# A gated linear-attention kernel with a low-rank expert layer: all queues ordered anew, four more decayed k on GpSimd, and the first r and k requested on ScalarE's queue

## The chip, the core and the metric

The program runs on one core of a Trainium2 chip. A core has five engines that run their own instruction queues in order: TensorE (PE, matrix products into PSUM; its weight loads are listed as PEld), VectorE (DVE), ScalarE (ACT), GpSimd (POOL) and SyncE (SP, which in this kernel only requests transfers). Sixteen DMA engines move data between memory and SBUF. The engines meet through semaphores. The metric is device time in microseconds, one launch, median of the runs.

## The reference

Inputs are r, k, v, w of shape (4 batches, 8 heads, 768 steps, 48), u of shape (8, 48), and the expert layer's w_gate (384 x 8), A (8 x 384 x 16) and B (8 x 16 x 384). For each batch and head a 48 x 48 state is carried over the steps:

```
for t in range(768):
    cur   = outer(u * k[t], v[t])
    y[t]  = r[t] @ (state + cur)
    state = w[t][:, None] * state + outer(k[t], v[t])
```

The y of the 8 heads are laid side by side: x has 3072 tokens of 384 numbers. Each token picks its two experts with the largest x @ w_gate, softmaxes these two logits, and the output is x + sum over the two of weight * (x @ A[e]) @ B[e].

## The kernel before

The 768 steps of a batch are cut into six tiles of 128 steps, so there are 24 tiles, numbered 0 to 23; all 8 heads of a tile are treated together, as four pairs. The recurrence becomes matrix work within a tile and a state that is passed from tile to tile. A tile t goes through these stages (the names are functions inside `tile_kernel`, and a name with a number, such as kmul.5, is that stage for that tile):

- loads: `load_rk` (r and k, 514 KB, one of a ring of 12 buffers), `load_w` (two tiles at a time, except that tiles 0 and 1 come singly), `load_v` (the first three tiles by SP in float32, then cast by `castv`; the later ones by GpSimd's own queue, several tiles at a time), `consts` (0: u, 1: aw, the gate and A side by side, 2: B), which `castc` turns to bf16
- decay: `ln` (ACT, logarithm of w), `cs` (PE, cumulative sums into the one PSUM buffer x_ps), `expp` and `expm` (ACT, exponentials of the sums and of their negatives; `expm` overwrites x_ps, or writes an SBUF tile em where the product after it is GpSimd's)
- products: `rmul` (GpSimd, r times the decay, tile rd), `qmul` (GpSimd, r times k, tile q), `kmul` (k times the inverse decay, the "decayed k", on VectorE or, for the tiles in K_ON_POOL, on GpSimd)
- scores: `amm` (PE, into the one PSUM buffer a_ps), `aev` (VectorE, multiplies by the causal mask, the costliest stage there; tile 23 does it in two halves, `aev` and `aev2`), `dgmm` and `dv` (the diagonal term with u)
- state: `ktr`, `ktev` (decayed k transposed, and copied out), `kv` (PE, adds to the state s_ps), `resc` (VectorE, every second tile), `sev` (a copy of the state)
- output of the attention: `ymd`, `ymS`, `ymv` (PE), `yev` (copy to xT)
- expert layer: `zl` (PE, gate and A for three tiles together), `top`, `gexp`, `gsel`, `gmul`, `gnorm`, `gmul2`, `zw` (choice of the two experts), `zT`, `zTev`, then per tile `dmm` (PE), `oev` (copy to res) and `store` (SP)
- `warm.n`: n matmuls of zeros that fill PE's idle time

Which instruction follows which on every engine is written out by hand in the string ORDER (L53 to L99): the program is issued in this order, and an engine runs its own stages in the order in which they stand there. Constants above it (L41 to L50) tell which engine takes a stage that two could do: K_ON_POOL, KT_ON_DVE, S_ON_DVE, OUT_ON_DVE, ZT_ON_ACT, V_ON_ACT and so on; L166 to L176 are the copies. PE's, VectorE's, ACT's and GpSimd's queues and SP's requests are all set in this way. A request on SP also waits until the request eight places before it has landed.

Of the kernel before, what the change touches and what calls it, by code (L numbers as in the profile page):

```python
# [23 lines left out]
HD = H * D  # L24
# [3 lines left out]
WL = 2  # L28
# [15 lines left out]
V_ON_ACT = (0, 1)  # L44
K_ON_POOL = (8, 9, 14, 17, 21, 22, 23)
KT_ON_DVE = (0, 6, 13, 16, 20)
S_ON_DVE = (1, 8, 18, 21)
Y_ON_DVE = (20,)
OUT_ON_DVE = (2, 10, 23)
ZT_ON_ACT = (2, 14, 17, 20)  # L50
# [11 lines left out]
yev.3 kv.3 resc.3 sev.3 dgmm.4 dv.4 amm.4 aev.4 gmul2.2 zw.2 qmul.6 cs.6 expp.6 ktr.4 ktev.4 expm.6 kmul.6
rmul.6 ymd.4 ymS.4 kv.4 sev.4 ymv.4 yev.4 dgmm.5 dv.5 load_v.9 zT.2 zTev.2 amm.5 aev.5 cs.7 dgmm.6 dv.6
ymd.5 consts.2 castc.2 dmm.1 expp.7 expm.7 load_v.12 load_rk.7 qmul.7 rmul.7 kmul.7 load_w.8 load_rk.8 ln.8
qmul.8 load_rk.9 load_w.10 load_rk.10 load_rk.11 load_w.12 load_rk.12 ymS.5 ymv.5 yev.5 ktr.6 ktev.6 amm.6
aev.6 oev.1 store.1 cs.8 expp.8 expm.8 rmul.8 kmul.8 dmm.0 oev.0 store.0 load_rk.13 load_w.14 load_rk.14
load_rk.15 load_w.16 load_rk.16 load_rk.17 dgmm.7 dv.7 ymd.6 zl.5 ymv.6 yev.6 kv.6 sev.6 top.5 gexp.5 gsel.5
amm.7 aev.7 ktr.7 ktev.7 cs.9 expp.9 expm.9 dmm.2 oev.2 store.2 gmul.5 gnorm.5 qmul.9 ln.10 ymd.7 ymS.7
dgmm.8 dv.8 gmul2.5 zw.5 ymv.7 yev.7 kv.7 resc.7 sev.7 amm.8 aev.8 ktr.8 ktev.8 zT.5 zTev.5 kmul.9 ymd.8
cs.10 expp.10 expm.10 ymS.8 dgmm.9 dv.9 kv.8 sev.8 ymv.8 yev.8 kmul.10 rmul.9 amm.9 aev.9 qmul.10 qmul.11  # L70
ktr.9 ktev.9 dmm.4 oev.4 store.4 rmul.10 dmm.3 oev.3 store.3 cs.11 expp.11 expm.11 rmul.11 dgmm.10 dv.10
zl.8 top.8 gsel.8 kv.9 resc.9 kmul.11 ln.12 gexp.8 gmul.8 gnorm.8 gmul2.8 ymd.9 ktr.10 ktev.10 ymS.9 ymv.9
yev.9 amm.10 aev.10 sev.9 qmul.12 cs.12 expp.12 expm.12 rmul.12 qmul.13 dmm.5 oev.5 dgmm.11 dv.11 qmul.14
ymd.10 ymS.10 ymv.10 yev.10 kv.10 sev.10 kmul.12 amm.11 load_w.18 load_rk.18 load_rk.19 load_w.20 load_rk.20
dgmm.12 qmul.15 ln.14 cs.13 expp.13 expm.13 rmul.13 zw.8 zT.8 ymd.11 ymS.11 aev.11 ymv.11 amm.12 yev.11
store.5 dv.12 ktr.12 ktev.12 zTev.8 dmm.7 oev.7 dmm.6 oev.6 store.6 kmul.13 aev.12 dgmm.13 dv.13 cs.14
expp.14 expm.14 rmul.14 ln.16 zl.11 top.11 gexp.11 load_v.18 ymd.12 ktr.13 ktev.13 gsel.11 gmul.11 amm.13
aev.13 ymv.12 yev.12 kv.12 kmul.14 cs.15 gnorm.11 gmul2.11 dgmm.14 dv.14 qmul.17 ymd.13 sev.12 kv.13 ymS.13
resc.13 expp.15 expm.15 rmul.15 dmm.8 oev.8 store.8 kmul.15 zw.11 ymv.13 yev.13 qmul.16 ktr.14 ktev.14
amm.14 aev.14 cs.16 ymd.14 zT.11 zTev.11 dgmm.15 dv.15 qmul.18 sev.13 ymS.14 store.7 expp.16 expm.16 rmul.16  # L80
kmul.16 load_rk.21 load_w.22 kv.14 ymv.14 yev.14 amm.15 dmm.10 oev.10 store.10 ln.18 ktr.15 ktev.15 aev.15
ymd.15 sev.14 cs.17 expp.17 expm.17 kmul.17 zl.14 top.14 gexp.14 dgmm.16 dv.16 ymS.15 kv.15 resc.15 gsel.14
gmul.14 ymv.15 yev.15 amm.16 aev.16 rmul.17 sev.15 gnorm.14 gmul2.14 cs.18 expp.18 expm.18 rmul.18 ktr.16
ktev.16 qmul.19 dmm.9 oev.9 ymd.16 kmul.18 ln.20 zw.14 ymS.16 ymv.16 yev.16 dgmm.17 dv.17 qmul.20 dmm.11
oev.11 store.11 kv.16 sev.16 amm.17 aev.17 cs.19 expp.19 expm.19 rmul.19 dgmm.18 dv.18 qmul.21 ymd.17
kmul.19 zT.14 zTev.14 load_rk.22 load_rk.23 ymS.17 ymv.17 yev.17 amm.18 aev.18 ktr.18 ktev.18 dmm.12 cs.20
# [515 lines left out]
```

## Time and profile before

| what | value |
|---|---|
| time, median of 3 runs | 87.56 us (87.2 to 87.73) |
| the profiled execution | 87.54 us |
| its span in the profile | 85.7 us |
| PE busy | 77.1 us (90%) |
| VectorE busy | 73.1 us (85%) |
| ScalarE busy | 70.5 us (82%) |
| GpSimd busy | 61.9 us (72%) |
| moved by DMA | 25.43 MB, mean 297 GB/s |

The span runs from the first instruction to the last; the time has the launch around it. Busy time counts an engine's own instructions without requests of transfers, and the ends of PE's matmuls are modelled. The last loads are requested at 60.8 us, so that from about 64 us on only stores are left. A row of the timeline is: start in us, length in us, engine, line, operation, output <- input, shapes, count, and in square brackets the idle time of that engine just before and whom it waited for. Tile names in rows: lw is the logarithm, ep and x_ps the two exponentials, rd and q GpSimd's products, kd with a number a decayed k, at the masked scores, sb the copied state, idle_ps the output of a `warm` matmul.

### The profile page before, as it was taken

The numbers are of one execution on the slowest core, as the hardware profiler recorded it, in microseconds if no ns is written. First come the engines' busy times: TensorE is split into PE (matmuls) and PEld (weight loads), VectorE is DVE, ScalarE is ACT, GpSimd is POOL, SyncE is SP. The second block draws the span as 40 slices with busy tenths as digits, with TensorE's granted clock in tenths as the row PEclk, the third lists the DMA queues.
The fourth block names the chain that finished last, engine by engine and source line by source line (L and its number), as shares of the span: only waits on it lengthen the run. The fifth ranks groups of instructions, "written<-read, shape, count | busy, mean of one in ns | idle before, by whom it ended". The sixth has DMA issues, their size and how long they took to land.

```text
span 85.7 us, 3410 instructions
## 1 busy us (share of the span) xinstructions
PE 77.1 (90%) x1354; PEld 56.8 (66%) x1354; DVE 73.1 (85%) x176; ACT 70.5 (82%) x156; POOL 61.9 (72%) x88
## 2 busy tenths in 40 slices
PE   4899999979999999999989999999999999999810
PEld 1226557567676987787778877877787778675400
DVE  5946559969999999999999999999997999957830
ACT  5275887958999999999989989999999886976500
POOL 6054978698899798896987999499965897822000
PEclk9999999999999999999999999999999999999998
DMA  1999999999999999999999999999995504202461
GB/s 30 339 360 376 409 410 304 387 398 352 336 407 419 324 288 259 357 418 402 417 412 390 418 416 256 286 403 369 323 363 193 191 11 183 92 15 92 184 228 47
DMA packets 10384, 25.43 MB, mean 297 GB/s; under 512 B 1280, under 2 KB 4992, under 8 KB 10368
## 3 DMA queue, kind: packets, MB, share of 16 engines
q1 hardware_dynamic: 9648, 23.15, 70.7%
q0 software_dynamic: 720, 2.06, 12.1%
q8 instruction: 10, 0.16, 0.8%
q14 instruction: 6, 0.05, 0.2%
HBM read 22.56 MB, written 4.72 MB: 318 GB/s over the span
## 4 chain that ended last, share of the span: by engine, by line
DVE 34%; PE 24%; DMA 11%; ACT 8%; issue 8%; SPq 6%; POOL 4%; DVEq 0%; POOLq 0%; ACTq 0%
DMA aw_f<-in_aw_dram 11%; DVE at L314 10%; DVE dv L299 5%; PE a_ps L307 4%; DVE zw L474 3%; PE y_ps L371 3%; PE kd L281 3%; PE z_ps L412 3%; SPq L193 3%; DVE s_ps L339 2%; POOL rd L263 2%; SPq L187 2%; PE x_ps L240 2%; PE d_ps L512 2%; PE d_ps L496 2%
## 5 line engine op out<-in xcount | busy, mean ns | idle before, releaser
L263 POOL TENSOR_TENSOR rd<-rk,ep 128x512 bf16<-128x512 f32 x24 | 26.2, 1092 | 5.1 <-ACT ep L248 4.9
L314 DVE TENSOR_TENSOR at<-a_ps,mask 128x1024 bf16<-128x1024 f32 x23 | 28.0, 1218 | 1.7 <-PE a_ps L307 1.5
L258 POOL TENSOR_TENSOR q<-rk 128x384 bf16<-128x384 f32 x24 | 20.7, 866 | 2.8 <-DMA rk<-in_rk_dram 2.1
L248 ACT ACTIVATE ep<-x_ps 128x512 f32<-128x512 f32 x24 | 14.7, 614 | 2.5 <-PE x_ps L242 1.3
L170 ACT CAST xT<-y_ps 128x512 bf16<-128x512 f32 x22 | 13.1, 595 | 0.5 <-PE y_ps L371 0.2
L240 PE MATMUL x_ps<-tri,lw 128*128 128x128 f16 x96 | 12.0, 227 | 0.4 <-ACT lw L230 0.4
L230 ACT ACTIVATE lw<-w_in 128x768 f16<-128x768 f32 (+1 forms) x13 | 10.5, 806 | 1.4 <-DMA w_in<-in_w_dram 1.3
L299 DVE TENSOR_TENSOR dv<-v_bf,kd 128x384 bf16<-128x384 bf16 x21 | 11.4, 542 | 0.1
L170 ACT COPY res<-d_ps 128x384 f32<-128x384 f32 x21 | 9.9, 493 | 0.8 <-PE d_ps L512 0.7
L254 ACT ACTIVATE x_ps<-x_ps 128x512 f32<-128x512 f32 x17 | 10.4, 614 | 0.0
L240 PEld LDWEIGHTS <-lw 128*128 128x128 f16 x96 | 7.8, 100 | 3.0 <-ACT lw L230 1.7
L355 PE MATMUL y_ps<-ident,dv 128*128 128x128 bf16 x94 | 9.2, 219 | 0.1
L164 PE MATMUL idle_ps<-zero 128*128 128x512 bf16 x18 | 7.9, 560 | 1.2 <-DVE zero L111 1.2
L371 PE MATMUL y_ps<-at,v_bf 128*48 128x128 bf16 x160 | 8.1, 221 | 0.5 <-DVE at L314 0.4
L512 PE MATMUL d_ps<-b_b,zT 128*128 128x384 bf16 x24 | 7.8, 327 | 0.4 <-DVE zT L168 0.3
L364 PE MATMUL y_ps<-rd,sb 48*48 48x128 bf16 x156 | 8.0, 220 | 0.1
L496 PE MATMUL d_ps<-ident,xT 128*128 128x96 bf16 x92 | 7.7, 206 | 0.0
L170 ACT COPY ks<-kd 128x384 bf16<-128x384 bf16 x15 | 7.3, 488 | 0.3
L371 PEld LDWEIGHTS <-v_bf 128*48 128x48 bf16 x168 | 5.7, 101 | 2.2 <-issue 0.6
L242 PE MATMUL x_ps<-ones,lw 128*128 128x128 f16 x48 | 7.0, 227 | 0.0
L412 PE MATMUL z_ps<-aw_b,xT 128*128 128x136 bf16 x92 | 6.7, 222 | 0.0
L355 PEld LDWEIGHTS <-dv 128*128 128x128 bf16 x96 | 6.2, 97 | 0.6 <-DVE dv L299 0.3
(184 smaller groups left out, 158.9 us busy)
## 6 DMA issues: line engine op xcount, KB each, us to landing
rk<-in_rk_dram SPq DMA_DIRECT2D x24, 514.0 KB, 9.3
out_dram<-res SPq DMA_DIRECT2D x23, 192.0 KB, 4.2
w_in<-in_w_dram SPq DMA_DIRECT2D x11, 384.0 KB, 9.9
v_bf<-in_v_dram POOLq DMA_DIRECT2D x2, 576.0 KB, 10.1
v_bf<-in_v_dram POOLq DMA_DIRECT2D x3, 288.0 KB, 7.4
w_in<-in_w_dram SPq DMA_DIRECT2D x2, 192.0 KB, 3.2
v_f<-in_v_dram SPq DMA_DIRECT2D x1, 384.0 KB, 6.1
aw_f<-in_aw_dram SPq DMA_DIRECT2D x1, 272.0 KB, 9.3
```

Of the source, the lines that this page charges most:

```text
L170: nc.scalar.copy(out=o, in_=i)
L230: nc.scalar.activation(out=lw[:, o:o + n, :, 0:D].rearrange("p c h d -> p (c h) d"), in_=w_in[:, 0:n].rearrange("p c (h d) -> p (c h) d", ...
L240: nc.tensor.matmul(x_ps[:, p, :], lhsT=lwof(t, p), rhs=tri, start=True, stop=t % WL == 0)
L248: nc.scalar.activation(out=ep[:, :, o + 1:o + L + 1], in_=st[t]["x"], func=ACT.Exp)
L254: nc.scalar.activation(out=em, in_=st[t]["x"], func=ACT.Exp, scale=-1.0)
L258: (nc.vector if t in Q_ON_DVE else nc.gpsimd).tensor_mul(q, st[t]["r"][:, 0:PQ], st[t]["k"][:, 0:PQ])
L263: (nc.vector if t in R_ON_DVE else nc.gpsimd).tensor_mul(rd, st[t]["r"], st[t]["ep"][:, :, 0:L])
L299: nc.vector.tensor_mul(o[:, :, 0:D], vseq[t], dg.to_broadcast([128, H, D]))
L314: nc.vector.tensor_mul(at.rearrange("s g p f -> s (g p) f"), st[t]["a_ps"].rearrange("s g p f -> s (g p) f"), mask.to_broadcast([128, H, L]))
L355: nc.tensor.matmul(st[t]["y"][p], lhsT=st[t]["dv"][:, 2 * p:2 * p + 2, :].rearrange("p a b -> p (a b)"), rhs=ident, start=(p == 0 or (t == ...
L371: nc.tensor.matmul(st[t]["y"][p][g * 64:g * 64 + D], lhsT=vseq[t][:, h, :], rhs=at, start=False, stop=(h >= H - 2 or (t == NT - 1 and h % ...
L512: nc.tensor.matmul(d_ps, lhsT=st[t]["zT"], rhs=b_b, start=(t == NT - 1), stop=True, skip_group_check=True)
```

## The change

ORDER is written anew as a whole, so every queue changes. With it go the constants: GpSimd makes the decayed k of tiles 5, 7, 9, 11, 13, 15, 17, 19, 21, 22, 23 (before: 8, 9, 14, 17, 21, 22, 23), so VectorE has 13 of them and no longer 17; VectorE copies 8 outputs to res and no longer 3; ACT has 17 state copies for 16, 5 copies of zT for 4; all three casts of the first v are GpSimd's (before: two ACT's). The request of r and k of tile 0 moves from SP's queue, where it was the second, to ACT's, where it stands ahead of the loading of ACT's function table. The buffers of w become 7. There are 20 `warm` matmuls for 18.

On SP the requests begin: w.0, u, w.1, v.0, rk.1, w.2, v.1, rk.2, aw, rk.3, w.4, rk.4, B, rk.5 (before: w.0, rk.0, w.1, u, v.0, rk.1, w.2, v.1, rk.2, rk.3, w.4, aw, rk.4, rk.5, w.6, rk.6, B). On PE the queue begins: warm.5 cs.0 warm.4 amm.0 warm.4 cs.1 dgmm.0 warm.3 ymd.0 ymv.0 ktr.0 warm.1 cs.2 (before: warm.5 cs.0 warm.4 amm.0 cs.1 dgmm.0 warm.3 ktr.0 warm.1 kv.0 ymd.0 dgmm.1 cs.2).

```diff
-V_ON_ACT = (0, 1)
-K_ON_POOL = (8, 9, 14, 17, 21, 22, 23)
-KT_ON_DVE = (0, 6, 13, 16, 20)
-S_ON_DVE = (1, 8, 18, 21)
-Y_ON_DVE = (20,)
-OUT_ON_DVE = (2, 10, 23)
-ZT_ON_ACT = (2, 14, 17, 20)
+V_ON_ACT = ()
+K_ON_POOL = (5, 7, 9, 11, 13, 15, 17, 19, 21, 22, 23)
+KT_ON_DVE = (0, 4, 13, 15, 16)
+S_ON_DVE = (3, 6, 21)
+Y_ON_DVE = (17,)
+OUT_ON_DVE = (1, 4, 6, 13, 16, 19, 20, 23)
+ZT_ON_ACT = (5, 11, 14, 17, 20)
...
-warm.5 load_w.0 load_rk.0 load_w.1 ln.0 cs.0 warm.4 expp.0 expm.0 rmul.0 consts.0 ln.1 load_v.0 castc.0
-qmul.0 load_rk.1 load_w.2 castv.0 qmul.1 load_v.3 kmul.0 amm.0 cs.1 expp.1 expm.1 ln.2 load_v.1 aev.0
-castv.1 dgmm.0 warm.3 dv.0 ktr.0 warm.1 ktev.0 kv.0 sev.0 ymd.0 kmul.1 rmul.1 dgmm.1 dv.1 cs.2 warm.2 expp.2
-expm.2 load_rk.2 qmul.2 rmul.2 kmul.2 load_rk.3 qmul.3 load_w.4 castv.2 amm.1 aev.1 ktr.1 ktev.1 ymv.0
-warm.1 yev.0 consts.1 castc.1 kv.1 resc.1 sev.1 load_v.6 cs.3 expp.3 expm.3 rmul.3 kmul.3 ln.4 load_rk.4
...
+warm.5 load_w.0 ln.0 cs.0 warm.4 expp.0 expm.0 load_rk.0 consts.0 rmul.0 load_w.1 castc.0 ln.1 qmul.0 kmul.0
+amm.0 warm.4 load_v.0 castv.0 cs.1 expp.1 expm.1 dgmm.0 warm.3 aev.0 load_rk.1 qmul.1 load_w.2 ln.2 dv.0
+ymd.0 ymv.0 yev.0 ktr.0 warm.1 kmul.1 cs.2 expp.2 expm.2 ktev.0 kv.0 dgmm.1 warm.3 sev.0 load_v.3 load_v.1
+castv.1 dv.1 ymd.1 load_rk.2 kmul.2 rmul.1 amm.1 aev.1 ktr.1 ktev.1 cs.3 expp.3 expm.3 castv.2 qmul.2 dgmm.2
+dv.2 consts.1 castc.1 load_rk.3 kmul.3 load_w.4 load_rk.4 ln.4 ymS.1 ymv.1 yev.1 rmul.2 load_v.6 kv.1 resc.1
...
-    nc.scalar.preload_act_table_set("natural_log_exp_and_others")
...
+    nc.scalar.dma_start(out=rks[0], in_=rk[0])
+    nc.scalar.preload_act_table_set("natural_log_exp_and_others")
...
-        w_in = wk.tile([128, WL, HD], F32, name="w_in", bufs=5)
+        w_in = wk.tile([128, WL, HD], F32, name="w_in", bufs=7)
...
-        nc.sync.dma_start(out=o, in_=rk[t])
+        if t:
+            nc.sync.dma_start(out=o, in_=rk[t])
```

More of the change, by code (lines that the diff above doesn't have):

```diff
@@ L62 @@
[L62 to L86, printed above, removed]
@@ L108, in tile_kernel @@
     pp = ctx.enter_context(tc.tile_pool(name="pp", bufs=1, space=PSUM))
+    rks = []
+    for i in range(RING):
+        t_ = const.tile([128, RKW], F32, name=f"rk{i}")
+        rks.append(t_)
+    nc.scalar.dma_start(out=rks[0], in_=rk[0])
+    nc.scalar.preload_act_table_set("natural_log_exp_and_others")
     zero = const.tile([128, 512], BF16)
@@ L145, in tile_kernel @@
     b_b = const.tile([128, HD], BF16, name="b_b")
-    rks = []
-    for i in range(RING):
-        t_ = const.tile([128, RKW], F32, name=f"rk{i}")
-        rks.append(t_)
     s_ps = pp.tile([128, P, D], F32, name="s_ps")
```

55 lines of the change are left out of this document (40 added, 15 removed).

## The prediction

> **What bounds the kernel now.** I read the page first, for the span, the busy shares and the chain of waits, then busy time by stretches, then the timeline of each engine in the first 19 us and around the places that the change touches.
>
> ```profile
> span 85.7 us, 3410 instructions
> PE 77.1 (90%) x1354; PEld 56.8 (66%) x1354; DVE 73.1 (85%) x176; ACT 70.5 (82%) x156; POOL 61.9 (72%) x88
> ...
> PE   4899999979999999999989999999999999999810
> ...
> DVE 34%; PE 24%; DMA 11%; ACT 8%; issue 8%; SPq 6%; POOL 4%; DVEq 0%; POOLq 0%; ACTq 0%
> DMA aw_f<-in_aw_dram 11%; DVE at L314 10%; DVE dv L299 5%; PE a_ps L307 4%; DVE zw L474 3%; PE y_ps L371 3%; PE kd L281 3%; PE z_ps L412 3%; SPq L193 3%; DVE s_ps L339 2%; POOL rd L263 2%; SPq L187 2%; PE x_ps L240 2%; PE d_ps L512 2%; PE d_ps L496 2%
> ```
>
> The span is 85.7 us and the profiled execution took 87.54 us, so 1.84 us lie around it; the median of the runs is 87.56, so the sum below, made against 87.54, stands for the median as well. No engine is busy all the time, and the chain of waits is spread over DVE (34%), PE (24%) and DMA (11%, all of it the load of aw). One share of an average hides three stages, so the next view is by stretch; its columns are the length, the busy us of PE, PEld, DVE, ACT and POOL (instruction counts in brackets), the clock, the DMA share and GB/s.
>
> ```profile
> 16.00:72.00 56.00, 53.80 (x1074) 43.52 (x1073) 53.87 (x123) 52.20 (x118) 49.24 (x63) 1.00 0.94 334
> 76.00:85.70 9.70, 5.24 (x71) 3.24 (x67) 5.17 (x20) 3.75 (x11) 0.44 (x2) 0.98 0.34 123
> ```
>
> Between 16 and 72 us VectorE is busy 53.87 of 56 us, PE 53.80, ACT 52.20 and GpSimd 49.24. That is a full pipeline: VectorE has 2.1 us of idle time to give, whatever is reordered. The last 9.7 us are a drain, one tile deep (VectorE 5.17 of 9.70). What is loose is the first stage, up to aev.3, the fourth masked product on VectorE at 18.57. Its rows, engine by engine (start, length, engine and line, operation; in brackets the idle time before it and what ended that):
>
> ```profile
> 3.28 0.52 ACT L230 ACTIVATE lw<-w_in 128x384 f16<-128x384 f32 x1 [1.27 <-DMA w_in<-in_w_dram]
> 7.98 0.60 ACT L248 ACTIVATE ep<-x_ps 128x512 f32<-128x512 f32 x1 [0.68 <-PE x_ps L242]
> 11.20 0.60 ACT L248 ACTIVATE ep<-x_ps 128x512 f32<-128x512 f32 x1 [0.31 <-PE x_ps L240]
> 11.69 0.59 ACT L254 ACTIVATE x_ps<-x_ps 128x512 f32<-128x512 f32 x1
> 13.71 0.60 ACT L248 ACTIVATE ep<-x_ps 128x512 f32<-128x512 f32 x1 [0.46 <-PE x_ps L242]
> 14.72 0.83 ACT L230 ACTIVATE lw<-w_in 128x768 f16<-128x768 f32 x1
> 16.04 0.60 ACT L248 ACTIVATE ep<-x_ps 128x512 f32<-128x512 f32 x1
> ```
> ```profile
> 12.32 0.69 DVE L268 TENSOR_TENSOR kd__249<-rk,x_ps 128x512 bf16<-128x512 f32 x1 [0.81 <-ACT x_ps L254]
> 18.57 1.23 DVE L314 TENSOR_TENSOR at<-a_ps,mask 128x1024 bf16<-128x1024 f32 x1 [0.72 <-PE a_ps L307]
> ```
> ```profile
> 6.91 0.29 PE L240 MATMUL x_ps<-tri,lw 128*128 128x128 f16 x1
> 7.87 1.44 PE L164 MATMUL idle_ps<-zero 128*128 128x512 bf16 x3
> 15.03 0.61 PE L164 MATMUL idle_ps<-zero 128*128 128x512 bf16 x2
> 18.14 0.40 PE L307 MATMUL a_ps<-rd,kd__313 48*128 48x128 bf16 x8 [0.56 <-POOL rd L263]
> ```
> ```profile
> 5.22 1.09 POOL L263 TENSOR_TENSOR rd<-rk,ep 128x512 bf16<-128x512 f32 x1 [2.90 <-ACT ep L248]
> 15.79 0.64 POOL L176 CAST aw_b<-aw_f 128x544 bf16<-128x544 f32 x1 [1.11 <-DMA aw_f<-in_aw_dram]
> 16.98 1.10 POOL L263 TENSOR_TENSOR rd<-rk,ep 128x512 bf16<-128x512 f32 x1
> ```
>
> Two things are to be seen. First, a loop through one PSUM buffer: the sums x_ps are made on PE, read by two exponentials on ACT (11.20, 11.69), multiplied on VectorE (12.32), and only then may PE write x_ps again; the next exponential follows at 13.71, so a turn takes 2.51 us. Second, GpSimd stood 1.1 us for aw and came to the product rd of tile 3 only at 16.98, although its exponential had begun at 13.71; PE's scores of tile 3 waited for it until 18.14, and aev.3 until 18.57.
>
> **The change part by part.** *Loads.* aw moves ahead of rk.3 and the fourth w, so it no longer ends last; the wait of 1.1 us goes, and GpSimd reaches rd of tile 3 as soon as that tile's exponential is there. *First r and k on ACT's queue.* Landings before, from the rows of the requests and the view of DMA issues, whose last number is us from issue to landing:
>
> ```profile
> 0.74 0.37 SPq L187 DMA_DIRECT2D w_in<-in_w_dram  x1
> 1.17 0.42 SPq L193 DMA_DIRECT2D rk<-in_rk_dram  x1
> ...
> 9.18 0.33 SPq L187 DMA_DIRECT2D w_in<-in_w_dram  x1
> ```
> ```profile
> 9.08 0.72 POOL L204 DMA_DIRECT2D v_bf<-in_v_dram  x1
> ```
> ```profile
> w_in<-in_w_dram SPq DMA_DIRECT2D x1, 192.0 KB, 2.5
> rk<-in_rk_dram SPq DMA_DIRECT2D x1, 514.0 KB, 3.9
> ...
> v_bf<-in_v_dram POOLq DMA_DIRECT2D x1, 288.0 KB, 7.3
> w_in<-in_w_dram SPq DMA_DIRECT2D x1, 384.0 KB, 10.5
> ```
>
> The first w, issued at 0.74, landed 2.5 us later, at 3.24, and ACT's logarithm began at 3.28: it waited for nothing else. rk.0 landed at 1.17 + 3.9 = 5.07, before its first use at 5.22, which waited for the exponential. So w is the late one of the two, and the change lets 514 KB run beside its 192 KB. Bounds: no loss if w's pieces all go first; 5.07 - 3.24 = 1.83 us if w ends together with rk.0. The same two bytes flowed one after the other at 514 KB in 1.83 us, 281 KB per us; with equal shares 192 KB of rk.0 pass by the time w is through, 192/281 = 0.7 us. I take **+0.7**. That queues do share the engines is in the rows: v, issued at 9.08 on GpSimd's queue, took 7.3 us while w, issued on SP at 9.18 behind a full queue, took 10.5. The request itself now stands on ACT ahead of the loading of its table; at 0.4 us, as on SP, it is hidden in the 1.27 us for which ACT stood idle before 3.28.
>
> The Trainium skill, page "DMA: Bandwidth & Descriptors", section "Queues, rings and completion order", says that each DMA engine goes round between the queues that have work, a packet at a time. The overtaking of w by v agrees with it; by this rule the first w cannot keep the engines to itself, and the sum would have something between my 0.7 and the upper bound of 1.83 in place of the lower bound.
>
> The 0.43 us (0.74 to 1.17) by which SP's later requests come sooner are worth nothing, and neither does it hurt that rk.2's request waits for rk.0's landing (the program uses a request's semaphore again eight requests later): the DMA engines have a queue that makes a w 10.5 us late.
>
> *Idle matmuls.* The order puts four of them between the scores of tile 0 and the sums of tile 1 (cs.1, at 6.91 before). Three of them took 1.44 us at 7.87, starting 0.43 apart (1.44 less 0.59 for the last to drain, over two); two took 0.61 at 15.03, which is 0.22 apart (one lasts 0.39). At the early rate four cost 4 x 0.43 = 1.71 us, at the late one 0.9. At this place the rows on both sides are early ones, so I take 1.7. PE runs its queue in order, so cs.1 waits, and behind it the exponential of tile 1: 7.98 + 1.7 = 9.7. Three more and one more stand ahead of cs.2, about as many as before.
>
> *The loop from there.* Tile 2's exponential comes at least one turn later, 9.7 + 2.5 = 12.2 (before 11.20); tile 3's at 14.7 (13.71). Then ACT has, ahead of tile 4's, the two exponentials (13.71 to 14.72, 1.01) and a logarithm with a copy to xT behind it (14.72 to 16.04, 1.32): 14.7 + 2.33 = 17.0, and also a state copy that before stood on VectorE. Its second exponential 0.5 later, the product of k 0.63 after that (11.69 to 12.32), 18.15; then aev.3 0.6 to 0.7 later: 18.8, **+0.25** against 18.57. So the 1.1 us wait for aw goes, rd of tile 3 would be there near 16.5, but the exponentials are late next, and they hold kmul.4, which stands in front of aev.3. Every step of this hangs on the first logarithm, so the 0.7 of w is added whole: **start +0.95**.
>
> *The middle, on the engine that is full.* VectorE's rows, one right behind the other, give each operation's price as start to start:
>
> ```profile
> 51.84 0.35 DVE L168 COPY zT<-zT_ps 128x384 bf16<-128x384 bf16 x1
> 52.11 0.55 DVE L299 TENSOR_TENSOR dv<-v_bf,kd 128x384 bf16<-128x384 bf16 x1
> 52.57 0.68 DVE L268 TENSOR_TENSOR kd__1475<-rk,x_ps 128x512 bf16<-128x512 f32 x1
> 53.19 0.56 DVE L168 COPY res<-d_ps 128x384 f32<-128x384 f32 x1
> 53.67 1.21 DVE L314 TENSOR_TENSOR at<-a_ps,mask 128x1024 bf16<-128x1024 f32 x1
> ...
> 76.29 0.69 DVE L322 TENSOR_TENSOR ath<-a_ps,mask 128x512 bf16<-128x512 f32 x1 [0.93 <-PE a_ps L307]
> ```
>
> A copy of zT 0.27, a dv 0.46, a decayed k 0.62, a copy of an output 0.48. Between aev.3 and the first half of the last masked product (76.29) VectorE loses four decayed k (-2.48), gains four output copies (+1.92), loses one zT copy (-0.27) and takes dv.23, which stood behind it (+0.46): **-0.4 us**. The state and ks copies come out even there. Behind 76.29 the dv goes and the output copy of tile 20 comes: nothing. Work moves, but VectorE, which is full, keeps it.
>
> *ACT* loses five output copies and two casts of v and gains a zT and a state copy:
>
> ```profile
> L170 ACT COPY res<-d_ps 128x384 f32<-128x384 f32 x21 | 9.9, 493 | 0.8 <-PE d_ps L512 0.7
> ```
>
> Five times 0.49 is 2.5 us less on an engine that is busy 52.2 of 56; it waits for PE and VectorE instead, so I count nothing. *GpSimd* gains four decayed k and two casts:
>
> ```profile
> 74.38 1.09 POOL L268 TENSOR_TENSOR kd__2149<-rk,em 128x512 bf16<-128x512 f32 x1
> ```
> ```profile
> 14.17 0.50 POOL L176 CAST v<-v_f 128x384 bf16<-128x384 f32 x1
> ```
>
> 4 x 1.09 = 4.4 us in the middle, and two casts of 0.5 at the start, which fit into its 2.9 us of idle time ahead of 5.22 and the wait for aw. It had 56 - 49.24 = 6.8 us idle in the middle; 2.4 stay. A decayed k that took 0.62 us on VectorE takes 1.09 here, but its exponential now goes to an SBUF tile, so x_ps is free sooner, by the length of that product. I count these two at nothing; bounds are in the rival. Two more buffers for w, the order of stores and the order of the drain: nothing, since no row of the middle waits for w, and the last chain runs through the same steps (scores, mask, gate, one store) at the same lengths.
>
> **Sum:** 87.54 + 0.95 - 0.4 = 88.1 us, 0.6% over the median.
>
> **The rivals.**
> *GpSimd becomes the bound* (slower). In the middle its idle time falls from 6.8 to 2.4 us, and two of the things it waited for, exponentials and the gate's sums, come in an order that it cannot pick. It decides where the waits that remain exceed 2.4 us. If all 6.8 came back, the end would be 4.4 us later; against it speaks that an engine that is later finds its inputs ready. A quarter of it, 1.1, gives 89.2 us.
>
> *The start gets shorter* (faster). If w keeps its 3.24 and the four idle matmuls run at the late rate, tile 1's exponential comes at 7.98 + 0.9 = 8.9 and aev.3 at 18.8 - 0.8 = 18.0, half a us sooner than now, with no wait behind it. In the middle VectorE's 2.1 us idle may shrink by half, because ACT has 2.5 us less to do and x_ps comes free sooner. 87.54 - 0.55 - 0.4 - 0.6 = 86.0 us. It decides at w's landing: with the first logarithm at 3.3 it can hold, at 4.0 not. The Trainium skill, page "TensorE: Matmul & The Clock Gate", section "Part 1: The HAM clock gate", has the array at its full rate after some 3.4 us of sustained work, by which the four would run at the late rate; this trace speaks against it, since PE is busy from the first slice on (4 8 9 9 tenths of 2.14 us each) and yet the idle matmuls at 7.87 are 0.43 us apart.
>
> *It moves nothing* (the same): w loses nothing, the four idle matmuls fall into a wait, VectorE keeps its pace: 87.54 - 0.4 = 87.1 us.
>
> **How the numbers follow.** Forecast 88.1: 0.40, with a range of its own of 87.5 to 88.9. GpSimd bound, 89.2: 0.22. Shorter start, 86.0: 0.25. Nothing moves, 87.1: 0.13. About 1% of 87.56, 0.9 us, is what a measurement tells from no change: 86.7 and 88.4 are the limits. Faster: 0.25 and a tenth of the last, 0.27. Slower: 0.20 and a third of the forecast's case, 0.35 together, 0.13 + 0.22. Same: 0.38. The range leaves out about a tenth on each side: below 86.0 half of the faster case, above 89.5 a third of the GpSimd case.
>
> **What would show it.** In the changed profile: the first logarithm at about 4.0 (3.3 says that w was not held up); four idle matmuls right behind the scores of tile 0, 1.7 us long; no GpSimd wait for aw; aev.3 at about 19.5; VectorE with nearly the same busy time and the drain of 9.4 us from the first half mask to the end unchanged; GpSimd near 67 us busy. I am wrong if aev.3 comes before 18, or if VectorE's idle time between aev.3 and the drain differs by more than a us from now.

## The result, and the profile after

The changed kernel takes 88.86 us (median of six runs, 87.88 to 89.49), the kernel before, measured beside it, 87.64 us (six runs, 87.2 to 88.33). The ratio is 1.013 with a 95% interval of 1.0084 to 1.0175: slower by 1.3%. The forecast was 88.1 in a range of 86.0 to 89.5, and the time lies in that range; the likeliest outcome (within 1%, 0.38) did not come, the next (slower by over 1%, 0.35) did. Ratios leave out executions that took over 1.5% longer than the kernel's fastest, which the medians include, and four of the kernels in the table further on (*before, aw and B early*, *sixth w first*, *w and aw as before*, *idle matmuls in the gap*) were profiled in such an execution, so that their rows are read for places and only roughly for sizes. The changed kernel's profiled execution took 88.83 us with a span of 87.1, so it stands for the median.

The page of the kernel after: its span, the busy time of each engine, and the chain of waits.

```profile
span 87.1 us, 3416 instructions
PE 75.8 (87%) x1356; PEld 56.1 (64%) x1356; DVE 72.9 (84%) x175; ACT 67.8 (78%) x151; POOL 66.7 (77%) x94
...
PE 30%; DVE 29%; ACT 13%; DMA 12%; issue 6%; POOL 5%; DVEq 0%; POOLq 0%; ACTq 0%
```

GpSimd rose from 61.9 to 66.7 us, ScalarE fell from 70.5 to 67.8, VectorE is where it was (73.1, now 72.9). The same stretches as before, after the change (columns as in the prediction; the drain begins at 77.3 now):

```profile
16.00:72.00 56.00, 53.65 (x1092) 43.34 (x1090) 53.90 (x120) 53.40 (x120) 52.57 (x67) 1.00 0.94 333
77.30:87.10 9.80, 4.95 (x76) 3.23 (x72) 5.52 (x21) 3.63 (x10) 0.44 (x2) 0.93 0.37 128
```

The middle is as full as it was (VectorE 53.90 of 56, before 53.87), with more of GpSimd in it (52.57, before 49.24). The drain's work is nearly unchanged too (VectorE 5.52 us, before 5.17). So the loss is in the start. VectorE's timeline after, at the masked products of tiles 3 and 5 and at the last one:

```profile
20.50 1.22 DVE L317 TENSOR_TENSOR at<-a_ps,mask 128x1024 bf16<-128x1024 f32 x1
...
26.92 1.22 DVE L317 TENSOR_TENSOR at<-a_ps,mask 128x1024 bf16<-128x1024 f32 x1
...
77.58 1.29 DVE L325 TENSOR_TENSOR ath<-a_ps,mask 128x512 bf16<-128x512 f32 x2
```

The product of tile 3 (aev.3) starts 1.93 us later (18.57 before), the last one 1.29 (76.29 before): between them 57.08 us instead of 57.72, so the middle gave back 0.64. From the last product to the end of the span it is 9.52 us, before 9.41. 1.93 - 0.64 + 0.11 = 1.40 us, which is the difference of the spans.

Where the 1.93 us come from is in ScalarE's timeline after:

```profile
0.73 0.40 ACTq L114 DMA_DIRECT2D rk<-in_rk_dram  x1
1.16 1.28 ACT L115 ACT_TABLE_LOAD   x1 [1.16 <-PEq L594]
5.42 0.52 ACT L233 ACTIVATE lw<-w_in 128x384 f16<-128x384 f32 x1 [2.98 <-DMA w_in<-in_w_dram]
...
11.38 0.60 ACT L251 ACTIVATE ep<-x_ps 128x512 f32<-128x512 f32 x1 [3.11 <-PE x_ps L245]
```

The first logarithm begins at 5.42 instead of 3.28: 2.14 us late, with the load of the first w as the releaser. The rest of the start is 0.21 us *shorter* than before (1.93 - 2.14). PE's timeline shows the four added idle matmuls and what stood behind them:

```profile
8.51 0.61 PE L310 MATMUL a_ps<-rd,kd__160 48*128 48x128 bf16 x8 [0.20 <-DVE kd__160 L271]
9.05 1.85 PE L166 MATMUL idle_ps<-zero 128*128 128x512 bf16 x4
10.73 0.23 PE L243 MATMUL x_ps<-tri,lw 128*128 128x128 f16 x1
...
11.26 0.81 PE L166 MATMUL idle_ps<-zero 128*128 128x512 bf16 x3
```

The sums of tile 1 begin 1.68 us after the start of the idle ones. From there PE is quicker than it was at the same place before: the eight matmuls of those sums took 0.45 us (10.73 to 11.18) where they took 0.83 (6.91 to 7.74), and the next three idle ones 0.81 where they took 1.44. In both traces the matmuls come closer together from about 10 us on, so what stands later in time is cheaper, and some 1.0 of the 1.68 us comes back there. GpSimd no longer stands for aw (its conversion follows the q ahead of it without a gap) and is at the decayed r of tile 3 at 17.03, where it was at 16.98 before, although all began 2.14 us later:

```profile
14.38 0.63 POOL L178 CAST aw_b<-aw_f 128x544 bf16<-128x544 f32 x1
...
17.03 1.08 POOL L266 TENSOR_TENSOR rd<-rk,ep 128x512 bf16<-128x512 f32 x1 [0.43 <-ACT ep L251]
```

### The profile page after: what moved, and what is told of

Same layout as the page of the kernel before. It is cut to its first block, busy times and chain, and to the rows that moved or that the text cites. A ratio compares the mean times of both kernels' runs of the same rounds, so it can differ in the third digit from the quotient of the medians.

```text
span 87.1 us, 3416 instructions
## 1 busy us (share of the span) xinstructions
PE 75.8 (87%) x1356; PEld 56.1 (64%) x1356; DVE 72.9 (84%) x175; ACT 67.8 (78%) x151; POOL 66.7 (77%) x94
## 4 chain that ended last, share of the span: by engine, by line
PE 30%; DVE 29%; ACT 13%; DMA 12%; issue 6%; POOL 5%; DVEq 0%; POOLq 0%; ACTq 0%
DVE at L317 9%; DMA out_dram<-res 7%; DMA w_in<-in_w_dram 5%; DVE dv L302 4%; PE a_ps L310 4%; PE idle_ps L166 4%; ACT ep L251 3%; PE x_ps L243 3%; PE kd L284 3%; ACT x_ps L257 3%; PE z_ps L415 3%; DVE zw L477 2%; PE y_ps L358 2%; PE d_ps L515 2%; POOL q L261 2%
## 5 line engine op out<-in xcount | busy, mean ns | idle before, releaser
L243 PE MATMUL x_ps<-tri,lw 128*128 128x128 f16 x96 | 11.5, 222 | 3.1 <-ACT lw L233 3.0
L172 ACT COPY res<-d_ps 128x384 f32<-128x384 f32 x16 | 7.8, 495 | 0.3
L257 ACT ACTIVATE x_ps<-x_ps 128x512 f32<-128x512 f32 x13 | 8.0, 617 | 0.0
L257 ACT ACTIVATE em<-x_ps 128x512 f32<-128x512 f32 x11 | 6.7, 608 | 0.0
```

Source lines behind the costliest of these rows:

```text
L172: nc.scalar.copy(out=o, in_=i)
L243: nc.tensor.matmul(x_ps[:, p, :], lhsT=lwof(t, p), rhs=tri, start=True, stop=t % WL == 0)
L257: nc.scalar.activation(out=em, in_=st[t]["x"], func=ACT.Exp, scale=-1.0)
```

## Experiments

Two theories stood. *Start*: the first w, slowed by the r, k beside it, and the idle matmuls cost some 2 us, and the middle can't earn them back. *GpSimd*: its eleven decayed k are the loss. The table gives each kernel's ratio to the kernel before, measured beside it, and from its profiled execution the start of the first logarithm and of the masked products of tiles 3 and 5 (us).

| kernel | ratio (95% interval) | first ln | tile 3 | tile 5 |
|---|---|---|---|---|
| before | 1 | 3.28 | 18.57 | 25.41 |
| after | 1.013 (1.008 to 1.018) | 5.42 | 20.50 | 26.92 |
| r, k on SP | 1.004 (0.999 to 1.009) | 3.25 | 19.60 | 26.81 |
| before, r, k on ACT | 1.005 (1.001 to 1.009) | 5.57 | 19.84 | 26.67 |
| no idle matmuls there | 1.000 (0.995 to 1.006) | 4.71 | 19.43 | 26.65 |
| request behind table | 1.009 (1.004 to 1.014) | 4.61 | 19.05 | 26.50 |
| k on VectorE again | 1.067 (1.056 to 1.078) | 3.15 | 19.08 | 26.34 |
| before, aw and B early | 1.012 (0.999 to 1.024) | 3.72 | 20.17 | 28.01 |
| sixth w first | 1.034 (1.026 to 1.043) | 3.41 | 20.74 | 29.15 |
| w and aw as before | 1.012 (1.003 to 1.020) | 3.23 | 19.18 | 27.57 |
| before, k on GpSimd | 1.037 (1.031 to 1.043) | 4.29 | 19.46 | 27.14 |
| idle matmuls in the gap | 0.999 (0.996 to 1.003) | 3.32 | 18.97 | 25.68 |
| loads in order | 1.001 (0.998 to 1.004) | 3.23 | 19.36 | 26.24 |
| all steps | 1.004 (1.000 to 1.008) | 3.27 | 18.57 | 25.37 |

**The first r, k back on SP** (in the changed kernel):

```diff
-    nc.scalar.dma_start(out=rks[0], in_=rk[0])
...
-        if t:
-            nc.sync.dma_start(out=o, in_=rk[t])
+        nc.sync.dma_start(out=o, in_=rk[t])
```

> The changed kernel with one part undone: r and k of tile 0 are again the second request on SP's queue. If the shared start of the two transfers is what delayed the first w (landed 5.33 us, before 3.24), the first logarithm starts at 3.3 again and everything behind it moves by about 2.1 us: aev.3 near 18.4, about 86.8 us, faster than the kernel before by 0.9%. If the new order of PE, ACT and GpSimd in the start is the cause, the time stays near 88.9.

Measured: 88.11 us, 1.004 of before, where the changed kernel had 1.013: better, but far from the expected 86.8. ScalarE's timeline of this run:

```profile
3.25 0.52 ACT L231 ACTIVATE lw<-w_in 128x384 f16<-128x384 f32 x1 [1.23 <-DMA w_in<-in_w_dram]
...
15.99 0.84 ACT L231 ACTIVATE lw<-w_in 128x768 f16<-128x768 f32 x1 [1.42 <-DMA w_in<-in_w_dram]
```

The first logarithm is back at 3.25, all of the 2.14 us. At tile 3 only 0.9 is left of it and at tile 5 0.1, because the fourth w, requested behind aw and r, k of tile 3, landed only when ScalarE had stood 1.42 us for it. PE stood with it, and what followed is in the stretches of this run (PEclk, the third column from the end, is the granted clock):

```profile
13.90:17.30 3.40, 1.45 (x36) 1.04 (x31) 2.62 (x5) 1.98 (x5) 3.38 (x4) 1.00 1.05 366
17.30:20.70 3.40, 3.34 (x48) 2.52 (x48) 1.79 (x2) 2.25 (x7) 1.99 (x3) 0.52 1.06 346
```

PE was busy 1.45 of 3.4 us, and for the next 3.4 us it was granted half its clock.

**That request alone, in the kernel before** (one line more, ahead of the table load, and SP leaves it out; the buffers of r and k are declared earlier for it):

```diff
+    nc.scalar.dma_start(out=rks[0], in_=rk[0])
...
-        nc.sync.dma_start(out=o, in_=rk[t])
+        if t:
+            nc.sync.dma_start(out=o, in_=rk[t])
```

> The kernel before with one part of the change alone: r and k of tile 0 requested on ACT ahead of the table load. By the theory of the shared start the first logarithm starts at about 5.4 us and the time rises by up to 2.1 us, to 89 to 89.8; less, if the waits for rk.1, w.2 and aw that follow in this order swallow a part, since those transfers do not land later. By the rival (the order is to blame) it stays near 87.6.

Measured: 88.59 us, 1.005, less than the 89 to 89.8 of the theory without its reservation. The first logarithm, in ScalarE's timeline:

```profile
5.57 0.52 ACT L233 ACTIVATE lw<-w_in 128x384 f16<-128x384 f32 x1 [3.12 <-DMA w_in<-in_w_dram]
```

2.29 us late at the first logarithm, 1.27 at tile 3, 1.33 at the last masked product (77.62 against 76.29). So the request on ScalarE's queue is a loss in the old order too; in this trace the pipeline takes in about half of the delay, and by the ratio 0.5% of the time is left.

**No idle matmuls between the scores of tile 0 and the sums of tile 1** (in the changed kernel, with the request on ACT):

```diff
-amm.0 warm.4 load_v.0 castv.0 cs.1
+amm.0 load_v.0 castv.0 cs.1
```

> The changed kernel without the four idle matmuls between the scores of tile 0 and the sums of tile 1. By the prediction's step they hold cs.1 back by 1.7 us: cs.1 starts at 9.1 instead of 10.73, and the time falls by up to 1.7 us if the loop of exponentials sets the start, to 87.2. Against it: without them the array may stay slow longer, and the idle matmuls further on cost 0.43 us each instead of 0.22; then less than 1 us is gained.

Measured: 88.44 us, 1.000; the interval ends below that of the changed kernel, though the expected 87.2 was not reached. Tile 3 came 1.07 us sooner, but 0.71 of that is the first logarithm, which was sooner in this run; of the 1.68 us of the idle matmuls 0.36 is left. PE's next idle matmuls show where the rest went:

```profile
9.29 1.44 PE L166 MATMUL idle_ps<-zero 128*128 128x512 bf16 x3
```

They took 1.44 us and not 0.81: without the four, PE stayed slow longer, as the second half of the expectation has it. Tile 5 came only 0.27 sooner. The logarithm of tile 6 in ScalarE's timeline shows the next wait:

```profile
22.82 0.84 ACT L233 ACTIVATE lw<-w_in 128x768 f16<-128x768 f32 x1 [0.72 <-DMA w_in<-in_w_dram]
```

The sixth w, requested behind aw, the third constant and r, k of tile 5, landed at 22.8, and it held ScalarE.

**The request on ACT behind the table load in program order:**

```diff
-    nc.scalar.dma_start(out=rks[0], in_=rk[0])
     nc.scalar.preload_act_table_set("natural_log_exp_and_others")
+    nc.scalar.dma_start(out=rks[0], in_=rk[0])
```

> The changed kernel with the request of r and k of tile 0 still on ACT, but behind the table load, so it starts about 1.3 us after the first w. If it is the common start that slows both, w lands near 3.3 to 3.6 us and the time is that of the kernel with the request on SP, about 86.8 to 87.2. If sharing at any time delays w, the first logarithm stays above 4.5 us and the time above 88.

Measured: 88.60 us, 1.009. The two rows of ScalarE say that the edit did not delay the request:

```profile
0.73 1.28 ACT L114 ACT_TABLE_LOAD   x1 [0.73 <-PEq L594]
0.77 0.39 ACTq L115 DMA_DIRECT2D rk<-in_rk_dram  x1
4.61 0.52 ACT L233 ACTIVATE lw<-w_in 128x384 f16<-128x384 f32 x1 [2.59 <-DVE s_ps L154]
```

The load of the table runs from 0.73 to 2.01, and the request behind it went out at 0.77, as early as without the edit. So a later start of that load wasn't tried; the run is one more sample of the common start. (The brackets name a fill by VectorE, L154, which ended at 4.56; the first w landed at 4.54 by the view of DMA issues, and with r, k on SP the logarithm began at 3.25, ahead of that fill. The wait is for w.)

That makes it the right kernel to compare with: it is in effect the changed one, and it was measured together with the three others. It has the four idle matmuls and its first logarithm at 4.61; the kernel without them has 4.71. Yet tile 3 comes at 19.05 here and at 19.43 there, and tile 5 at 26.50 and 26.65. The four took 1.05 us here, from 8.24 to the sums of tile 1 at 9.29 (the row's 1.21 counts the last one's end, which overlaps them):

```profile
8.24 1.21 PE L166 MATMUL idle_ps<-zero 128*128 128x512 bf16 x4
```

The medians of these kernels are 88.60 us here, 88.11 with r, k on SP and 88.44 without the idle matmuls. So r, k on SP is worth about 0.5 us; that leaving out the idle matmuls is a gain, the traces don't show, and the median shows 0.16 us of it.

**Four decayed k back on VectorE** (the kernel with r, k on SP; tiles 5, 11, 15, 19):

```diff
-K_ON_POOL = (5, 7, 9, 11, 13, 15, 17, 19, 21, 22, 23)
+K_ON_POOL = (7, 9, 13, 17, 21, 22, 23)
```

> The changed kernel with the first r, k as the second request of SP's queue (as in the first experiment, 1.004 of before), and four of the eleven decayed k (tiles 5, 11, 15, 19) back on VectorE, so that it has seven on GpSimd, as many as before. Theory 'GpSimd is not the bound, the loads of the first 25 us are': VectorE gets 4 x 0.68 us more and loses 4 x 1.09 us of GpSimd's, no gain: 0 to +1.5 us against the first experiment, ratio to before 1.004 to 1.02, and the span from the fifth masked product (tile 5) to the last product of the drain longer by up to 1.5 us. Rival 'GpSimd, with eleven, has become the bound': GpSimd's waits of PE for the decayed r go, 0.5 to 1.5 us faster than the first experiment, ratio 0.987 to 0.998.

Measured: 93.56 us, 1.067, nearly four times the most that I had allowed for. The rows of VectorE and PE around tile 11:

```profile
39.48 0.69 DVE L269 TENSOR_TENSOR kd__997<-rk,x_ps 128x512 bf16<-128x512 f32 x1 [1.38 <-ACT x_ps L255]
...
41.02 1.21 DVE L315 TENSOR_TENSOR at<-a_ps,mask 128x1024 bf16<-128x1024 f32 x1
```
```profile
40.69 0.38 PE L282 MATMUL kd<-ident,kd__926 128*128 128x128 bf16 x4 [1.44 <-DVE dv L300]
```

The order written for GpSimd has the decayed k of tile 11 ahead of dv.10 and of the masked product of tile 10. On VectorE, which works in the order of the program, it made both wait for the exponential of tile 11 (1.38 us), and PE for dv (1.44). So the run neither confirms nor refutes the rival (GpSimd as the bound): it prices the position of the products, not the move.

**The same move the other way, in the kernel before:**

```diff
-K_ON_POOL = (8, 9, 14, 17, 21, 22, 23)
+K_ON_POOL = (5, 8, 9, 11, 14, 15, 17, 19, 21, 22, 23)
```

> The kernel before with nothing changed but the engine of four decayed k: tiles 5, 11, 15 and 19 on GpSimd, so that it has eleven, as many as the changed kernel. Theory 'that part is a gain of the middle by itself': VectorE gives 4 x 0.68 = 2.7 us, GpSimd takes 4 x 1.09 = 4.4 us of the 7 us that it has free, the whole is 0.3 to 1 us faster (ratio 0.988 to 0.997). Rival 'moved without a new order it costs, since GpSimd works its instructions in order and has the product of r and the q of the next tile behind it, as four k moved the other way cost 5.5 us in the changed order': 1 to 4 us slower, ratio 1.01 to 1.045.

Measured: 91.13 us, 1.037. VectorE and PE, where the added products stand on GpSimd:

```profile
23.44 0.18 DVE L458 TENSOR_REDUCE den<-pe 128x3 f32<-128x24 f32 x1 [1.71 <-POOL pe L452]
```
```profile
66.36 0.40 PE L307 MATMUL a_ps<-rd,kd__1742 48*128 48x128 bf16 x8 [0.85 <-POOL kd__1742 L268]
```

VectorE waits 1.71 us for the gate's product pe, which stands behind the decayed k of tile 5 on GpSimd, and PE 0.85 us for the decayed k of tile 19. By the medians the same four products cost 3.4 us here (against the kernel before, measured beside it) and some 5.5 there (against r, k on SP, measured at another time): in both, the order fits only the split that it was made for.

**The order of SP's requests, in the kernel before** (aw right behind r, k of tile 2; B, the third constant, right behind those of tile 4; here and in the next experiments the lines show only SP's requests out of ORDER, unless other stages stand beside them):

```diff
-load_rk.2 load_rk.3 load_w.4 consts.1 load_rk.4 load_rk.5 load_w.6 load_rk.6 consts.2
+load_rk.2 consts.1 load_rk.3 load_w.4 load_rk.4 consts.2 load_rk.5 load_w.6 load_rk.6
```

> The kernel before with nothing changed but two requests on SP's queue: aw right behind r, k of tile 2 (ahead of tile 3's and of the fourth w), and the third constant right behind r, k of tile 4 (ahead of tile 5's and of the sixth w), as the changed kernel has them. Theory 'the order of SP's requests costs, since the first 25 us live from the loads': the fourth and the sixth w land 0.6 to 2 us later, the logarithms of tiles 4 and 6 wait for them, the masked product of tile 3 comes earlier than 18.57 (GpSimd has aw sooner), but that of tile 5 at 26.0 to 27 instead of 25.41, and the whole is 0.5 to 1.2 us slower than before (ratio 1.006 to 1.014). Rival 'aw's early request is a gain, as the prediction had it (its wait of 1.1 us on GpSimd goes, and 0.25 us of it stays)': 0.3 to 0.7 us faster, ratio 0.992 to 0.997.

Measured: 89.56 us, 1.012, with an interval that reaches to 0.999. ScalarE's logarithm of tile 4:

```profile
16.79 0.84 ACT L228 ACTIVATE lw<-w_in 128x768 f16<-128x768 f32 x1 [1.40 <-DMA w_in<-in_w_dram]
```

It began at 14.72 before and waited for nothing. aw early is no gain by itself: what it takes is the time of the fourth w. Tile 3, which the theory had earlier than 18.57, came later (20.17).

**The sixth w ahead of r, k of tile 5** (kernel with r, k on SP; B behind r, k of tile 6, its conversion just ahead of its use):

```diff
-load_rk.4 consts.2 load_rk.5 load_w.6 load_rk.6
+load_rk.4 load_w.6 load_rk.5 load_rk.6 consts.2
```

> The first experiment (changed kernel, first r, k on SP) with the sixth w asked for ahead of r, k of tile 5, and the third constant only behind r, k of tile 6 (its conversion on ScalarE moved to just ahead of its first use). Theory 'all variants of the changed order come to the masked product of tile 5 at 26.5 to 26.9 because the sixth w lands at 22.7': it lands 1.5 to 2.5 us earlier, the masked product of tile 5 starts at 25.3 to 26.0, and the time falls by 0.6 to 1.2 us against the first experiment (ratio to before 0.990 to 0.997). Rival 'the dip at tile 5 comes from the engines' order, not from that load': the product of tile 5 stays at 26.5 to 27 and the time within 0.3 us of the first experiment.

Measured: 90.62 us, 1.034, and tile 5 at 29.15: the expectation failed in both its branches, since the time is well above the kernel without the edit. ScalarE and VectorE:

```profile
17.11 0.84 ACT L230 ACTIVATE lw<-w_in 128x768 f16<-128x768 f32 x1 [1.81 <-DMA w_in<-in_w_dram]
```
```profile
15.69 0.69 DVE L268 TENSOR_TENSOR kd__306<-rk,x_ps 128x512 bf16<-128x512 f32 x1 [0.54 <-DMA rk<-in_rk_dram]
```

Now the fourth w and r, k of tile 3 are late. Whether the sixth w landed sooner did not come to matter.

**All w and aw in the order of the kernel before** (as the last, with the fourth w ahead of r, k of tile 3 and of aw, aw's conversion behind the decayed r of tile 2, and without the four idle matmuls):

```diff
-load_rk.2 consts.1 load_rk.3 load_w.4 load_rk.4
+load_rk.2 load_w.4 load_rk.3 consts.1 load_rk.4
```

> As the experiment with the sixth w first, and beside it the fourth w ahead of r, k of tile 3 and of aw, aw's conversion on GpSimd behind the decayed r of tile 2, and without the four idle matmuls between the scores of tile 0 and the sums of tile 1. Theory 'loads in the order in which they are needed': the logarithm of tile 4 waits no longer, the masked product of tile 3 comes at 18.0 to 19.0, that of tile 5 at 24.5 to 25.5, the clock does not fall between 16 and 24 us, and the kernel takes 0.98 to 0.993 of before. Rival 'the start is bound by the loop of exponentials, not by loads': tile 3 at 19.0 to 20.0, tile 5 at 25.5 or later, ratio 0.997 to 1.005.

Measured: 89.21 us, 1.012, outside what theory and rival allow. GpSimd and VectorE:

```profile
16.18 0.64 POOL L175 CAST aw_b<-aw_f 128x544 bf16<-128x544 f32 x1 [1.81 <-DMA aw_f<-in_aw_dram]
```
```profile
18.53 0.69 DVE L267 TENSOR_TENSOR kd__359<-rk,x_ps 128x512 bf16<-128x512 f32 x1 [1.34 <-DMA rk<-in_rk_dram]
```

The fourth w is in time, and aw (1.81 us) and r, k of tile 4 (1.34) are not. Each order of the loads that was tried has another last one. The theory "loads in the order of need" fell. Of the rival, the places held (tile 3 at 19.18, tile 5 at 27.57) and neither its ratio nor its reason. The clock, which the theory had at full rate, fell here too (0.51 from 16.2 to 23.1 us).

**Idle matmuls in the gap** (kernel with r, k on SP):

```diff
-amm.2 aev.2 cs.4
+amm.2 warm.6 aev.2 cs.4
```

> The first experiment (changed kernel, first r, k on SP's queue) with six idle matmuls between the scores of tile 2 and the sums of tile 4, where PE stood 1.55 us for the fourth w. Theory 'what the first experiment lost behind that wait it lost by the clock, which fell to 0.50 for some 4 us after it': the granted clock stays at 1.00 up to 30 us, the masked product of tile 5 starts 0.3 to 1.0 us before 26.81, the time is 0.3 to 1.0 us below the first experiment (ratio to before 0.993 to 1.001). Rival 'the clock is no loss, since the loads set the pace there': the masked product of tile 5 at 26.6 to 27.1, ratio 1.002 to 1.006.

Measured: 87.69 us, 0.999 of before. The stretches that had the half clock, and the logarithm of tile 4, which still waits for the fourth w, though it begins 0.48 us sooner than in the kernel without these matmuls (15.51, there 15.99):

```profile
13.90:17.30 3.40, 2.70 (x45) 1.89 (x46) 2.78 (x5) 2.35 (x6) 3.38 (x5) 1.00 1.07 320
17.30:20.70 3.40, 3.37 (x70) 2.59 (x68) 2.33 (x5) 3.19 (x7) 2.51 (x4) 1.00 1.07 360
```
```profile
15.51 0.84 ACT L230 ACTIVATE lw<-w_in 128x768 f16<-128x768 f32 x1 [0.84 <-DMA w_in<-in_w_dram]
```

PE is busy 2.70 of 3.4 us, the clock stays at 1.00, and tile 5 comes at 25.68, 1.1 us sooner; up to 0.5 of that can be the sooner w. By the times the gain is 0.45% with intervals that overlap; by the trace the expectation holds up to tile 5.

**Loads in the order of use, and two v later** (kernel with r, k on SP; three idle matmuls in the gap, the third constant's conversion moved to its first use):

```diff
-load_rk.2 consts.1 load_rk.3 load_w.4 load_rk.4 consts.2 load_rk.5 load_w.6
+load_rk.2 load_w.4 consts.1 load_rk.3 load_rk.4 load_w.6 load_rk.5 consts.2
...
-sev.0 load_v.3 load_v.1 castv.1
+sev.0 load_v.1 castv.1
-castv.2 qmul.2
+castv.2 load_v.3 qmul.2
-rmul.2 load_v.6
+rmul.2
-rmul.4
+rmul.4 load_v.6
```

> The first experiment with three idle matmuls at that place and the loads in the order of their use: the fourth w ahead of aw and of r, k of tile 3, the v of tiles 3 to 5 asked for one GpSimd conversion later and those of tiles 6 to 8 two products later, the sixth w ahead of r, k of tile 5 and of the third constant, whose conversion on ScalarE stands behind the transposed k of tile 6. Theory 'up to 25 us the supply is the bound (the sixteen DMA engines are full from 2 us on), so 0.6 MB of v asked for later bring the rest forward': the logarithm of tile 4 starts before 15.0, the masked product of tile 3 at 18.0 to 19.0, that of tile 5 at 24.8 to 25.8, ratio to before 0.985 to 0.997. Rival 'whatever is moved, another load is the last, and the engines stand for that': tile 3 at 19 to 20.5, tile 5 at 26 to 28, ratio 1.00 to 1.015.

Measured: 87.78 us, 1.001. No load is waited for by more than 0.2 us between 12 and 27 us, but GpSimd's request of v now stands in front of q and the decayed r of tile 2, and PE waits for them:

```profile
13.86 0.23 PE L285 MATMUL kd<-ub,q 128*128 128x8 bf16 x3 [0.75 <-POOL q L257]
15.47 0.40 PE L306 MATMUL a_ps<-rd,kd__261 48*128 48x128 bf16 x8 [0.61 <-POOL rd L262]
```
```profile
12.90:16.30 3.40, 1.88 (x41) 1.40 (x40) 2.59 (x5) 2.88 (x6) 3.38 (x5) 1.00 1.04 408
16.30:19.70 3.40, 3.40 (x40) 2.35 (x40) 1.85 (x3) 1.56 (x3) 2.69 (x5) 0.50 1.06 321
```

The clock fell again, after a stretch with 1.88 of 3.4 us busy and no gap of over 0.75 us. Tile 3 (19.36), tile 5 (26.24) and the ratio are the rival's numbers; its reason, another load that is last, is not what these rows show.

**All steps together** (the last kernel, with the v of tiles 3 to 5 at its old place, aw's conversion behind the decayed r of tile 3, and two idle matmuls more):

```diff
-castv.2 load_v.3 qmul.2 dgmm.2
+castv.2 qmul.2 warm.2 dgmm.2
...
-castc.1 rmul.2 rmul.3
+rmul.2 rmul.3 castc.1
```

> The experiment before this one with three more steps against the gaps that it showed: the v of tiles 3 to 5 asked for at its old place again (GpSimd stood there anyway for the v of tile 1), aw's conversion on GpSimd behind the decayed r of tile 3 instead of ahead of that of tile 2, and two idle matmuls ahead of the dots of tile 2, where PE stood 0.75 us for the q of tile 2. Theory 'with the loads in order it is GpSimd's sequence and the clock that hold the start': the scores of tile 2 begin at 14.2 to 14.8 instead of 15.47, the granted clock stays at 1.00, the masked product of tile 3 comes at 17.6 to 18.6, that of tile 5 at 24.6 to 25.6, ratio to before 0.983 to 0.995. Rival 'another load is the last again': tile 3 at 19 or later, tile 5 at 26 or later, ratio 0.998 to 1.005.

Measured: 88.36 us, 1.004. Up to tile 5 the trace is what the theory asked for (18.57, 25.37, clock 1.00). Then a load that had been put off, the v of tile 6, is the last, in VectorE's timeline:

```profile
27.47 0.55 DVE L299 TENSOR_TENSOR dv<-v_bf,kd 128x384 bf16<-128x384 bf16 x1 [0.88 <-DMA v_bf<-in_v_dram]
```

Tile 6 starts at 28.21, behind 27.54 of the kernel with idle matmuls in the gap. The ratio, 1.004, is the rival's. No kernel of the set is measurably faster than the one before.

## Why the prediction was right or wrong, step by step

**The first w.** The mechanism was right, the size was not. This is the step that failed: +0.7 with an upper bound of 1.83, measured +2.14. The step took equal shares of the engines, counted in bytes, at the rate of two loads that follow each other. The view of DMA queues (packets, MB, share of the engines; q1 is SP's queue, q10 ScalarE's), in the changed kernel from 3.0 to 3.5 us and from 3.6 to 3.98, has other shares:

```profile
q1 hardware_dynamic: 26, 0.04, 41.1%
q10 hardware_dynamic: 16, 0.07, 32.0%
...
q10 hardware_dynamic: 31, 0.13, 81.6%
q1 hardware_dynamic: 29, 0.04, 27.3%
```

The queues move about as many packets (55 and 47), but r, k get 0.20 MB and SP's queue 0.08: a row of r, k is 4 KB (514 KB in 128 rows) and a row of w 1.5. If a packet of the one went for each packet of the other, all of r, k would pass before w is through, 514/281 = 1.83 us; that is an estimate, and it is the prediction's upper bound and not its 0.7. The bound in turn took the two loads as ending together no later than r, k had ended before, so that the engines move as much as they did. They didn't: the third microsecond, after and before (last column GB/s),

```profile
2.00:3.00 1.00, 1.00 (x4) 0.30 (x2) 0.89 (x3) 0.44 (x1) 0.29 (x1) 1.00 0.54 100
```
```profile
2.00:3.00 1.00, 1.00 (x4) 0.30 (x2) 0.89 (x3) 0.02 (x1) 0.29 (x1) 1.00 0.93 302
```

has 100 instead of 302 GB/s. r, k landed later as well: at 0.73 + 5.0 = 5.73 by the view of DMA issues (5.07 before). Four runs with the common start have the first logarithm at 5.42, 5.57, 4.71 and 4.61, and 100 to 146 GB/s in that microsecond; the ten without it have 3.15 to 4.29 (the next to last 3.72) and 255 to 335 GB/s. Trainium skill, page "DMA: Bandwidth & Descriptors", section "Queues, rings and completion order": each engine goes round between the queues that have work; the late w agrees with it, the fall of the total to a third does not follow from it, and no run here shows its cause.

**The idle matmuls.** 1.7 forecast, 1.68 measured in the profiled execution; that it fits so well is luck in part. The prediction's early rate of 0.43 us holds only until PE speeds up, and that moment differs between executions: the same four cost 1.05 us with the request behind the table and 1.00 with r, k on SP (6.88 to 7.88). And what they delay is cheaper afterwards, which the step did not count (it took the idle matmuls ahead of cs.2 to cost as much as before).

**The start behind them.** +0.25 forecast for the idle matmuls and the loop together, -0.21 measured; PE's quicker matmuls behind 10.73 gave back 1.0 us, more than this difference, and how much of it reaches aev.3 isn't shown. That the wait for aw goes was right, and so was that it doesn't show at the end. That the loop of exponentials is late next was right for after, where VectorE works without a gap from 19.90 on; but once the start is repaired, it isn't the loop that is late: the fourth or sixth w, r, k of tile 3 or 4, aw or v is, whichever the order of requests put back (the waits named in six of the experiments). The prediction weighed that order for aw alone; it is the second limit of the first 25 us.

**The middle.** -0.4 by counting VectorE's operations, -0.64 measured; -0.42 of it lies between tiles 3 and 5, -0.22 behind. The drain held: 9.4 forecast, 9.52. One execution of each kernel stands behind these tenths.

**GpSimd and ScalarE at nothing.** The busy time (67 forecast, 66.7) was right, and the middle, which did not get longer, agrees with counting both engines at nothing. That this belongs to the order, and that the same four products cost 3.4 and some 5.5 us when moved without it, was in no step.

**The sum** came near because terms offset each other: +1.44 at the first w, -0.46 in the rest of the start, -0.24 in the middle, against the forecast of 88.1: 88.83 in the profiled execution (the 0.11 of the drain and 0.11 less outside the span cancel). So it is luck in part that the time lies 0.8 us from the forecast: one term alone was off by 1.4. Of the marks that the prediction set, the first logarithm (about 4.0, measured 5.42) and aev.3 (about 19.5, measured 20.50) were missed, the first by that term alone, the second mainly; the idle matmuls, the wait for aw, GpSimd's busy time and the drain came as told.

**The rivals.** *GpSimd becomes the bound* gave 89.2, nearest by number, but not by cause: the middle was not longer (57.08 us, before 57.72). The two experiments with four decayed k moved don't test it, since the order around them was made for another split. *The start gets shorter* fell at its own mark, the first logarithm. *Moves nothing* fell with it.

**How much is shown.** The request on ScalarE's queue delays the first w in either order and costs about 0.5%: 1.005 alone in the kernel before, and 1.009 against 1.004 in the changed one, all measured together. What is left of the loss is the rest of the new order, 0.4% with an interval that reaches 1 (0.999 to 1.009). What stays open is why the engines move so little when both queues start, and what leaving out the idle matmuls is worth: the ratio (1.000) makes it the whole loss, the median 0.16 us of it, and the traces nothing. The two repairs together, with nothing else changed, weren't tried; the kernel that had both also had other requests, and took 1.012.

## What to carry to other kernels

Where the first computation hangs on one small load, nothing should start beside it, on another queue either: here the load with the longer rows got most of the bytes, and the price was three times that of an equal share. Where the loads fill the engines, putting one forward puts another back: look for the next wait before moving a request. An order written out by hand and its split between engines are one choice: change them together or not at all. And a comparison of two traces needs a third of the same kind: here the same start differed by up to 1 us from one execution to the next.

## What the runs showed of the hardware

The granted clock fell to 0.50 for one stretch of 3.4 us in two kernels whose rows stand above, after a stretch of the same length in which PE was busy 1.45 and 1.88 us; it did not after 2.70. The longest gap before the fall was 1.55 us in one and 0.75 in the other. Trainium skill, page "TensorE: Matmul & The Clock Gate", section "Part 1: The HAM clock gate": the rate is halved or full, decided over windows of some 3.4 us. The halves and the length agree. Filling the gap with six idle matmuls kept the clock at 1.00.

At the start of the kernel PE's idle matmuls are slow too, though the view has the clock at 1.00 there: three took 1.44 us at 9.29 in the run without the four idle ones, and 0.81 at 9.81 in the run with the request behind the table. When PE becomes quick differs between executions of nearly the same start.

Two queues that start together moved 100 to 146 GB/s in the third microsecond (four runs), one queue 255 to 335 (ten runs). The load of ScalarE's table (0.73 to 2.01 us) does not hold back a DMA request that stands behind it (0.77).
